# Scheduler priority for the scores and the reads of a batch in an attention-then-MLP kernel

## The chip, the cores and the metric

The kernel runs on one core of a Trainium2 chip. The metric is the device time of one execution in microseconds (us). A core has five engines that run side by side, each through its own list of instructions in a fixed order: TensorE (PE in the profile; its weight loads are PEld), VectorE (DVE), ScalarE (ACT), GpSimd (POOL) and SyncE (SP, which here issues most of the DMAs). An instruction waits until the work of other engines on which it depends is done, and everything behind it on its engine waits too.

## What is computed

Eight batches (B = 8) with eight heads (H = 8) of 512 tokens (S) and 32 memory states (Ns) of width 64 (D). Each token attends to the states and each state to the tokens; the results, 544 rows of 512 for each batch, go through a two-layer MLP with a squared ReLU (512 to 2048 to 512).

```python
scores = scale * np.matmul(x, state.transpose(0, 1, 3, 2))
...
a /= a.sum(-1, keepdims=True) + 1e-09
xread = np.matmul(a, state)
scores2 = scale * np.matmul(state, x.transpose(0, 1, 3, 2))
...
a2 /= a2.sum(-1, keepdims=True) + 1e-09
sread = np.matmul(a2, x)
...
h = x @ w_in
r = np.maximum(h, 0.0)
g = r * r
return (g @ w_out).astype(np.float32)
```

## The kernel before

**The MLP's products.** Every large product is made of three products of split operands (hi times hi, hi times lo, lo times hi), each with 128x128 weights and 512 columns. The token rows of a batch never exist as `xread`: since `xread` is the product of `a` and `state`, the kernel multiplies `state` with `w_in` first. This gives `z` (line 154, a product with 64x32 weights, in pieces of 512 columns), which is split into `z_hi` and `z_lo`. A unit of the MLP is then `ph` (line 362: six matmuls of `z` with the softmax `a_hi`, `a_lo`), its ReLU `r` on ACT (line 367), the square into `ph` on DVE (line 375), the cast `g_hi` on ACT (line 84) and the rest `g_lo` on DVE (line 87), and two units later the second layer, `po` (line 405: twelve matmuls, eight with `g_hi` and four with `g_lo`). A batch has 16 units.

**The attention of a batch.** Among these stand, once for each batch: `scores` (line 203: eight products `pst` with 64x32 weights in float32, each recorded by the profile as two matmuls), the copy `keep` of `pst` on ACT (line 217), the softmax over the states on DVE and ACT (`turn1` to `turn2`, lines 245 to 278), the softmax over the tokens (`exps2`, lines 225 to 233), the transposes `pt` of the latter (line 311) and `read` (line 323: 32 products `pr` with 128x32 weights in float32, two matmuls each, and then the multiplication `rd` on DVE, line 328).

**Buffers.** PSUM has four buffers for `po`, two for `ph` and one (tag `px`) that `pst`, `pt`, `pr` and the pieces of `z` take in turns: each of them has to wait until the one before has been read out. `g_hi` and `g_lo` have two buffers each.

**What sets the order.** The units of the first part, up to the second visit of batch 0, are ordered by the planner in `begin` and stay as written. Everything behind is recorded unit by unit; `Ahead` spreads the steps of the attention over the units by their due times. A scheduler then orders what was recorded, engine by engine, by its own estimate of when each instruction can start and by priority, which is the place in the recording. It orders single instructions, so that the eight products of `scores` or the 32 of `read` may come apart. `tc.high_priority(offset=HURRY)` with `HURRY = 120` (line 129) lets the instructions in it count as recorded that much earlier. Before the change it stands around the pieces of `z` alone (line 608).

Of the kernel before, what the change touches and what calls it, by code (L numbers as in the profile page):

```python
# [18 lines left out]
def memory_attention_then_relu2_ffn(  # L19
# [21 lines left out]
    nc = tc.nc  # L41
    P = 128
    B, S, C = xn.shape
    D = stP.shape[1] // 2
    H = C // D
    N = stP.shape[2] // (H // 2)
    DM, DF = w_out.shape[1] // 2, w_out.shape[0]
    R = S + N
    NG = H * N // P
    HG = H // NG  # L50
    NCC = DM // P
    NFC = DF // P
    NT = S // P
# [75 lines left out]
    HURRY = 120  # L129
# [38 lines left out]
    state = {}  # L168

    def attention(b):  # L170
        NJ = S // 32
        pair, my = [], {}
# [24 lines left out]

        def scores():
            pst = ps_x.tile([P, NG, S], F32, name="pst", tag="px")
            for j in range(HG):  # L200
                for g in range(NG):
                    rows = slice(g * D, (g + 1) * D)
                    nc.tensor.matmul(  # L203
                        pst[j * N:(j + 1) * N, g, :], lhsT=state[b][rows, j, :],
                        rhs=my["t"][rows, j, :], start=True, stop=True,
                    )
            my["pst"] = pst
            my["q1"] = sb.tile([P, NG, NJ, N], F32, name="q1", bufs=1)
            my["m1"] = sb.tile([P, NG, NJ, 1], F32, name="m1", bufs=2)
            my["s1"] = sb.tile([P, NG, NJ, 1], F32, name="s1", bufs=2)  # L210
            my["at"] = sb.tile([P, NG, S], F32, name="at", bufs=1)
            my["nm2"] = sb.tile([P, NG], F32, name="nm2", bufs=2)
            my["e2"] = sb.tile([P, NG, S], F32, name="e2", bufs=LATE)
            my["s2"] = sb.tile([P, NG], F32, name="s2", bufs=2 * LATE)
# [101 lines left out]

        def read():
            pr = ps_x.tile([P, NG, S], F32, name="pr", tag="px")
            for g in range(NG):
                for t in range(NT):  # L320
                    for j in range(HG):
                        h = g * HG + j
                        nc.tensor.matmul(  # L323
                            pr[j * N:(j + 1) * N, g, :D], lhsT=my["e"][:, g, t, j * N:(j + 1) * N],
                            rhs=my["n"][:, t, h * D:(h + 1) * D], start=t == 0, stop=t == NT - 1,
                        )
            rd = sb.tile([P, NG, D], F32, name="rd", bufs=1)
            nc.vector.tensor_mul(  # L328
                out=rd, in0=pr[:, :, :D], in1=my["s2"].rearrange("p (g o) -> p g o", o=1)
                .broadcast_to([P, NG, D])  # L330
            )
            at = (b % GB) * N
            for j in range(HG):
                nc.gpsimd.tensor_copy(  # L334
                    out=sr[b // GB][at:at + N, j * NG * D:(j + 1) * NG * D],
                    in_=rd[j * N:(j + 1) * N].rearrange("p g d -> p (g d)"),
                )

        steps = dict(
            pad=pad, load_t=load_t, scores=scores, keep=keep, exps2=exps2, load_n=load_n, turn=turn,  # L340
            read=read,
        )
        return pair, steps, [soft(gs) if b < 2 else grouped(*soft(gs)) for gs in halves]
# [558 lines left out]
```

## Time and profile before

| | us |
|---|---|
| median of 3 runs | 684.58 (684.29 to 684.79) |
| the profiled execution | 684.99 |
| its span, first to last instruction | 682.8 |
| PE busy | 653.2 (96%) |
| DVE busy | 368.8 (54%) |
| ACT busy | 289.7 (42%) |
| mean granted TensorE clock | 0.998 |

A busy PE says that a matmul was under way, not that it went at its best rate: matmuls overlap, so their durations add up to more than the time they take. What a matmul costs in a full stream is read from the distance between two starts. In the timeline, the first column is the start in us from the beginning of the span, the second the time until the last of the row's instructions ended, then the engine, the line, the operation with its tiles, weights and shape, and the number of instructions in the row.

### The profile page before, as it was taken

The page shows a single profiled execution, that of the slowest core. Times are in us where ns is not written, and L with a number is a line of the kernel's source. Part 1 is how long each engine was busy: PE and PEld are TensorE (multiplying, and loading weights), DVE is VectorE, ACT ScalarE, POOL GpSimd, SP SyncE. Part 2 cuts the span into 40 slices and gives each one's busy share as a digit, 9 for nine tenths or more (in the row PEclk, how much of TensorE's full clock was granted, in tenths as well). Part 3 has the DMA queues.
Part 4 walks back from the last instruction along what each step waited for, and adds up shares of the span by engine and source line. Part 5 has one row for each costly group of instructions (what it writes and reads, how often), then busy time and mean ns, then how long its engine had stood idle before and what let it go on. Part 6 is the DMA issues. An engine that isn't in the chain of part 4 may idle for free.

```text
span 682.8 us, 9542 instructions
## 1 busy us (share of the span) xinstructions
PE 653.2 (96%) x3864; PEld 493.7 (72%) x3864; DVE 368.8 (54%) x522; ACT 289.7 (42%) x468; POOL 24.3 (4%) x44
## 2 busy tenths in 40 slices
PE   1798999999999999999999999999999999999996
PEld 0465876777777777777777876777678767788895
DVE  4899789347557335633473336633483244343553
ACT  3667665334435333523343334423353143333442
POOL 0000000000101000100001000100001000000000
PEclk9999999999999999999999999999999999999999
DMA  8534560023130005000320005000301001000101
GB/s 315 185 127 182 184 232 24 1 70 121 47 138 5 1 1 186 4 1 1 117 69 5 1 1 186 0 1 1 124 0 63 1 0 62 1 0 1 62 1 31
DMA packets 15803, 43.59 MB, mean 64 GB/s; under 512 B 1296, under 2 KB 3344, under 8 KB 13840
## 3 DMA queue, kind: packets, MB, share of 16 engines
q1 hardware_dynamic: 15568, 42.73, 17.3%
q8 instruction: 30, 0.49, 0.3%
q10 hardware_dynamic: 192, 0.26, 0.2%
q14 instruction: 13, 0.11, 0.0%
HBM read 34.08 MB, written 8.91 MB: 63 GB/s over the span
## 4 chain that ended last, share of the span: by engine, by line
PE 90%; DVE 6%; issue 1%; ACT 1%; DMA 1%; SPq 0%; DVEq 0%; ACTq 0%
PE po L405 53%; PE ph L362 28%; PE pz L154 4%; PE pst L203 2%; PE pr L323 1%; PE pt L311 1%; DMA xt_raw<-xT 1%; DVE wof L114 1%; DVE wo_lo L87 1%; DVE z_lo L87 1%; DVE wi L114 1%; DVE wi L120 1%; DVE a_lo L87 0%; DVE q L275 0%; DVE m L251 0%
## 5 line engine op out<-in xcount | busy, mean ns | idle before, releaser
L405 PE MATMUL po<-wo_hi,g_hi 128*128 128x512 f32 x544 | 215.8, 397 | 0.1
L405 PE MATMUL po<-wo_lo,g_hi 128*128 128x512 f32 x544 | 213.9, 393 | 0.8 <-DVE wo_lo L87 0.8
L375 DVE TENSOR_TENSOR ph<-ph,r 128x512 f32<-128x512 f32 (+1 forms) x128 | 84.9, 663 | 138.5 <-ACT r L367 138.4
L367 ACT ACTIVATE r<-ph 128x512 f32<-128x512 f32 (+1 forms) x144 | 82.9, 575 | 177.1 <-PE ph L362 176.7
L405 PE MATMUL po<-wo_hi,g_lo 128*128 128x512 f32 x544 | 154.3, 393 | 0.0
L87 DVE TENSOR_TENSOR g_lo<-ph,g_hi 128x512 fp32r<-128x512 f32 (+1 forms) x144 | 94.8, 658 | 80.4 <-ACT g_hi L84 55.7
L84 ACT CAST g_hi<-ph 128x512 fp32r<-128x512 f32 (+1 forms) x144 | 81.2, 564 | 116.1 <-DVE ph L375 76.8
L405 PEld LDWEIGHTS po<-wo_hi,g_hi 128*128 128x128 f32 x544 | 102.3, 188 | 31.9 <-ACT r L367 5.9
L405 PEld LDWEIGHTS po<-wo_lo,g_hi 128*128 128x128 f32 x544 | 102.2, 188 | 27.5 <-issue 5.0
L405 PEld LDWEIGHTS po<-wo_hi,g_lo 128*128 128x128 f32 x544 | 100.7, 188 | 24.8 <-issue 3.8
L362 PE MATMUL ph<-a_hi,z_hi 128*128 128x512 f32 x256 | 83.9, 409 | 2.6 <-ACT a_hi L84 1.8
L362 PE MATMUL ph<-a_hi,z_lo 128*128 128x512 f32 x256 | 82.6, 402 | 3.4 <-DVE z_lo L87 3.4
L362 PE MATMUL ph<-a_lo,z_hi 128*128 128x512 f32 x256 | 80.7, 397 | 0.0
L362 PEld LDWEIGHTS ph<-a_hi,z_hi 128*128 128x128 f32 x256 | 47.1, 191 | 25.3 <-issue 5.8
L87 DVE TENSOR_TENSOR z_lo<-pz,z_hi 128x1024 fp32r<-128x1024 f32 (+2 forms) x37 | 39.7, 1077 | 46.0 <-ACT z_hi L84 46.0
L362 PEld LDWEIGHTS ph<-a_hi,z_lo 128*128 128x128 f32 x256 | 48.4, 191 | 20.2 <-issue 5.0
L362 PEld LDWEIGHTS ph<-a_lo,z_hi 128*128 128x128 f32 x256 | 48.9, 191 | 10.9
L84 ACT CAST z_hi<-pz 128x1024 fp32r<-128x1024 f32 (+2 forms) x37 | 32.9, 899 | 48.1 <-PE ph L362 26.7
L154 PE MATMUL pz<-wi,sp_raw 64*32 64x512 f32 (+2 forms) x560 | 36.4, 579 | 10.6 <-DVE wi L120 8.6
L154 PEld LDWEIGHTS pz<-wi,sp_raw 64*32 64x32 f32 x560 | 6.5, 107 | 25.1 <-DVE wi L120 10.2
L334 POOL COPY sr<-rd 32x128 f32<-32x128 f32 x32 | 9.2, 288 | 377.0 <-DVE rd L328 376.0
L203 PE MATMUL pst<-xt_raw,sp_raw 64*32 64x512 f32 x128 | 13.7, 658 | 6.6 <-DMA xt_raw<-xT 6.6
(61 smaller groups left out, 383.8 us busy)
## 6 DMA issues: line engine op xcount, KB each, us to landing
xt_raw<-xT SPq DMA_DIRECT2D x8, 1024.0 KB, 4.8
wo_raw<-w_out SPq DMA_DIRECT2D x8, 1024.0 KB, 5.6
xn_raw<-xn SPq DMA_DIRECT2D x8, 1024.0 KB, 5.4
out<-sum SPq DMA_DIRECT2D x32, 256.0 KB, 3.9
wi_raw<-w_in SPq DMA_DIRECT2D x7, 1024.0 KB, 4.8
wi_raw<-w_in SPq DMA_DIRECT2D x2, 512.0 KB, 6.7
sp_raw<-stP SPq DMA_DIRECT2D x8, 64.0 KB, 1.8
out<-os__5348 SPq DMA_DIRECT2D x2, 64.0 KB, 1.7
```

The source lines that it names most:

```text
L84: nc.scalar.copy(out=hi, in_=src)
L87: eng_lo.tensor_sub(out=lo, in0=src, in1=hi.bitcast(F32))
L114: nc.vector.scalar_tensor_tensor(out=bits, in0=high, scalar=-0x80000000, in1=bits, op0=ALU.bitwise_and, op1=ALU.bitwise_or,)
L120: mark[:] = [nc.vector.scalar_tensor_tensor(out=bits, in0=low, scalar=29, in1=bits, op0=ALU.logical_shift_right, op1=ALU.bitwise_or,)]
L154: nc.tensor.matmul(pz[g][j * N:(j + 1) * N], lhsT=state[b][rows, j, :], rhs=wi[rows, j, cols], start=True, stop=True,)
L203: nc.tensor.matmul(pst[j * N:(j + 1) * N, g, :], lhsT=state[b][rows, j, :], rhs=my["t"][rows, j, :], start=True, stop=True,)
L311: nc.tensor.transpose(out=pt[:, g, t, :], in_=my["e2"][:, g, t * P:(t + 1) * P], identity=ident)
L334: nc.gpsimd.tensor_copy(out=sr[b // GB][at:at + N, j * NG * D:(j + 1) * NG * D], in_=rd[j * N:(j + 1) * N].rearrange("p g d -> p (g d)"),)
L362: nc.tensor.matmul(ph, lhsT=w, rhs=v, start=m == 0, stop=m == len(todo) - 1)
L367: nc.scalar.activation(r, my[0], AF.Relu)
L375: nc.vector.tensor_mul(out=ph, in0=ph, in1=r)
L405: nc.tensor.matmul(po[t], lhsT=g, rhs=w, start=i == 0 and j == 0, stop=i == last and j == 2)
```

## The change

The loops of matmuls in `scores` and in `read` are put into `tc.high_priority(offset=HURRY)`. Nothing else is touched; the same instructions are issued. The lines behind shift by one and by two (203 to 204, 323 to 325, 362 to 364, 405 to 407).

```diff
         def scores():
             pst = ps_x.tile([P, NG, S], F32, name="pst", tag="px")
-            for j in range(HG):
-                for g in range(NG):
-                    rows = slice(g * D, (g + 1) * D)
-                    nc.tensor.matmul(
-                        pst[j * N:(j + 1) * N, g, :], lhsT=state[b][rows, j, :],
-                        rhs=my["t"][rows, j, :], start=True, stop=True,
-                    )
+            with tc.high_priority(offset=HURRY):
+                for j in range(HG):
+                    for g in range(NG):
+                        rows = slice(g * D, (g + 1) * D)
+                        nc.tensor.matmul(
+                            pst[j * N:(j + 1) * N, g, :], lhsT=state[b][rows, j, :],
+                            rhs=my["t"][rows, j, :], start=True, stop=True,
+                        )
...
         def read():
             pr = ps_x.tile([P, NG, S], F32, name="pr", tag="px")
-            for g in range(NG):
-                for t in range(NT):
-                    for j in range(HG):
-                        h = g * HG + j
-                        nc.tensor.matmul(
+            with tc.high_priority(offset=HURRY):
+                for g in range(NG):
+                    for t in range(NT):
+                        for j in range(HG):
+                            h = g * HG + j
+                            nc.tensor.matmul(
...
```

**The read, on PE.** This is what stands on PE around the read of batch 2 before, with the numbers of the buffers behind the names (`pr_2019` is the read, `ph_1992` a unit's first layer, `po0` to `po3` the four rows of its second):

```order
L405 MATMUL po3_1529<-wo_hi_76,g_lo_1912 128x512
L323 MATMUL pr_2019<-xn_raw_1967,e_t_1990 32x64 x8
L362 MATMUL ph_1992<-a_hi_1506,z_hi_1876 128x512 x2
L362 MATMUL ph_1992<-a_hi_1506,z_lo_1877 128x512 x2
L362 MATMUL ph_1992<-a_lo_1507,z_hi_1876 128x512 x2
L323 MATMUL pr_2019<-xn_raw_1967,e_t_1990 32x64 x24
L405 MATMUL po0_1526<-wo_hi_76,g_hi_1937 128x512
```

The same place of PE after the change:

```order
L407 MATMUL po3_1529<-wo_hi_76,g_lo_1912 128x512
L325 MATMUL pr_2019<-xn_raw_1967,e_t_1990 32x64 x32
L364 MATMUL ph_1992<-a_hi_1506,z_hi_1876 128x512 x2
L364 MATMUL ph_1992<-a_hi_1506,z_lo_1877 128x512 x2
L364 MATMUL ph_1992<-a_lo_1507,z_hi_1876 128x512 x2
L407 MATMUL po0_1526<-wo_hi_76,g_hi_1937 128x512
```

The 32 products stand in one piece, and `ph_1992` behind all of them. The reads of batches 2 to 5 were split like this, 8 and 24; those of the other batches are whole before and after.

**The scores, on PE.** One second layer further on, before the change, come the scores of batch 4 (`pst_2115`). Six of them stand behind `ph_2083`:

```order
L362 MATMUL ph_2083<-a_hi_1506,z_hi_1876 128x512 x2
L362 MATMUL ph_2083<-a_hi_1506,z_lo_1877 128x512 x2
L362 MATMUL ph_2083<-a_lo_1507,z_hi_1876 128x512 x2
L203 MATMUL pst_2115<-xt_raw_2097,sp_raw_2081 32x512 x6
L405 MATMUL po0_2099<-wo_hi_76,g_hi_1963 128x512
```

The other two stand on PE behind the twelve products of the next second layer, of which the last two are shown:

```order
L405 MATMUL po3_2102<-wo_lo_77,g_hi_1963 128x512
L405 MATMUL po3_2102<-wo_hi_76,g_lo_1964 128x512
L203 MATMUL pst_2115<-xt_raw_2097,sp_raw_2081 32x512 x2
L362 MATMUL ph_2131<-a_hi_1506,z_hi_1876 128x512 x2
L362 MATMUL ph_2131<-a_hi_1506,z_lo_1877 128x512 x2
```

After the change, on PE at the first of these places:

```order
L364 MATMUL ph_2083<-a_hi_1506,z_hi_1876 128x512 x2
L364 MATMUL ph_2083<-a_hi_1506,z_lo_1877 128x512
L204 MATMUL pst_2115<-xt_raw_2097,sp_raw_2081 32x512 x8
L364 MATMUL ph_2083<-a_hi_1506,z_lo_1877 128x512
L364 MATMUL ph_2083<-a_lo_1507,z_hi_1876 128x512 x2
L407 MATMUL po0_2099<-wo_hi_76,g_hi_1963 128x512
```

All eight scores now stand together, in the middle of `ph_2083`. The scores of batches 4 to 7 were split like this, 6 and 2; those of batches 0 to 3 are whole before and after. In all, pieces of small products stand at 69 places of PE's list before and at 61 after. Behind each of the four places, some pieces of `z` and some `ph` stand a few matmuls earlier or later, each still in one piece; in the last batches a `pt` that was split 2 and 6 is split 6 and 2.

**What follows from the scores, on DVE.** Before, DVE takes the transposition of the scores (`q1_2124`) behind the square and the rest of the unit `ph_2083`:

```order
L87 TENSOR_TENSOR g_lo_2003<-ph_1992,g_hi_2002 128x512
L375 TENSOR_TENSOR ph_2083<-ph_2083,r_2090 128x512
L87 TENSOR_TENSOR g_lo_2094<-ph_2083,g_hi_2093 128x512
L245 STREAM_TRANSPOSE q1_2124<-pst_2115 128x1024
L225 TENSOR_REDUCE nm2_2128<-e2_2129 128x2
L375 TENSOR_TENSOR ph_2131<-ph_2131,r_2138 128x512
L251 TENSOR_REDUCE m1_2125<-q1_2124 128x32
```

After the change DVE has there:

```order
L87 TENSOR_TENSOR g_lo_2003<-ph_1992,g_hi_2002 128x512
L246 STREAM_TRANSPOSE q1_2124<-pst_2115 128x1024
L226 TENSOR_REDUCE nm2_2128<-e2_2129 128x2
L377 TENSOR_TENSOR ph_2083<-ph_2083,r_2090 128x512
L252 TENSOR_REDUCE m1_2125<-q1_2124 128x32
L227 TENSOR_SCALAR nm2_2128<-nm2_2128 128x2
L87 TENSOR_TENSOR g_lo_2094<-ph_2083,g_hi_2093 128x512
```

The chain of the scores moved ahead of one unit's square and rest. On ACT the copy `keep` moved ahead of the ReLU and the cast of the same unit (`r_2090`, `g_hi_2093`). The lists of POOL and SP are the same before and after.

More of the change, by code (lines that the diff above doesn't have):

```diff
@@ L318, in read @@
             pr = ps_x.tile([P, NG, S], F32, name="pr", tag="px")
-            for g in range(NG):
-                for t in range(NT):
-                    for j in range(HG):
-                        h = g * HG + j
[L323 to L326, printed above, removed]
+            with tc.high_priority(offset=HURRY):
[4 more added lines that the diff above has]
+                            nc.tensor.matmul(
+                                pr[j * N:(j + 1) * N, g, :D], lhsT=my["e"][:, g, t, j * N:(j + 1) * N],
+                                rhs=my["n"][:, t, h * D:(h + 1) * D], start=t == 0, stop=t == NT - 1,
+                            )
             rd = sb.tile([P, NG, D], F32, name="rd", bufs=1)
```

## The prediction

> **What bounds the kernel now.** I read the page's shares first, then PE's waits without the start, and then how PE's time goes in the stretch where the change moves anything.
>
> ```profile
> PE 653.2 (96%) x3864; PEld 493.7 (72%) x3864; DVE 368.8 (54%) x522; ACT 289.7 (42%) x468; POOL 24.3 (4%) x44
> PE 90%; DVE 6%; issue 1%; ACT 1%; DMA 1%; SPq 0%; DVEq 0%; ACTq 0%
> PE ph L362 <- DVE z_lo L87: 1.1, 1, 1.1
> PE pz L154 <- DVE z_lo L87: 0.4, 1, 0.4
> 240.00:540.00 300.00, 300.00 (x1859) 223.48 (x1858) 143.91 (x202) 114.96 (x182) 16.55 (x28) 1.00 0.12 43
> ```
>
> The second line is the chain that ended last: 90% PE. The third and fourth are all that PE waited for others after 110 us (1.5 us in two waits). The last is the busy time from 240 to 540 us, where all four changed places lie: PE 300.00 of 300 us at a granted clock of 1.00, DVE and ACT under half. So here the end is set by how many matmuls PE starts and at what distance; a gain is a start-to-start distance that goes away, and nothing else is worth anything unless PE begins to wait.
>
> **The price of a step.** In the rows quoted below, 22 matmuls of 128x512 start between 268.37 and 273.41 (four of `ph`, then twelve and six of `po`): 5.04/22 = 0.229 us each. What a piece of small products costs is the distance around it, less 0.229 for each large matmul in that distance.
>
> **The reads.** A read in one piece, of batch 0, and then the split one of batch 2:
>
> ```profile
> 149.99 1.08 PE L405 MATMUL po<-wo_hi,g_lo 128*128 128x512 f32 x4
> 151.00 1.10 PE L323 MATMUL pr<-xn_raw,e_t 128*32 128x64 f32 x64
> 152.03 0.74 PE L362 MATMUL ph<-a_hi,z_hi 128*128 128x512 f32 x2
> 152.61 0.63 PE L362 MATMUL ph<-a_hi,z_lo 128*128 128x512 f32 x2
> ```
>
> ```profile
> 254.77 1.08 PE L405 MATMUL po<-wo_hi,g_lo 128*128 128x512 f32 x4
> 255.78 0.43 PE L323 MATMUL pr<-xn_raw,e_t 128*32 128x64 f32 x16
> 256.14 0.73 PE L362 MATMUL ph<-a_hi,z_hi 128*128 128x512 f32 x2
> 256.71 0.62 PE L362 MATMUL ph<-a_hi,z_lo 128*128 128x512 f32 x2
> 257.17 0.63 PE L362 MATMUL ph<-a_lo,z_hi 128*128 128x512 f32 x2
> 257.72 0.88 PE L323 MATMUL pr<-xn_raw,e_t 128*32 128x64 f32 x48
> 258.53 0.50 PE L405 MATMUL po<-wo_hi,g_hi 128*128 128x512 f32 x1
> 258.87 0.39 PE L405 MATMUL po<-wo_lo,g_hi 128*128 128x512 f32 x1
> ```
>
> Whole: 149.99 to 152.61 is 2.62; six large matmuls are 1.37; the read costs 1.25. Its body is 1.03 (151.00 to 152.03); the rest is paid at the borders: 151.00 is 0.09 later than four steps, and the two `ph` behind take 0.58 for 0.46. Split: 254.77 to 256.71 is 1.94, less 1.37 = 0.57; 257.17 to 258.87 is 1.70, less three steps (0.69) = 1.01; together 1.58. **One read made whole saves 0.33 us**, a pair of borders and 0.14 of body.
>
> **The scores.** Scores in one piece, inside a `ph`, of batch 2:
>
> ```profile
> 156.96 0.40 PE L362 MATMUL ph<-a_hi,z_hi 128*128 128x512 f32 x1
> 157.29 1.09 PE L203 MATMUL pst<-xt_raw,sp_raw 64*32 64x512 f32 x16
> 158.31 0.50 PE L362 MATMUL ph<-a_hi,z_hi 128*128 128x512 f32 x1
> 158.65 0.63 PE L362 MATMUL ph<-a_hi,z_lo 128*128 128x512 f32 x2
> ```
>
> The split ones of batch 4, and the unit `ph_2159` that comes later at 273.41:
>
> ```profile
> 262.31 0.62 PE L362 MATMUL ph<-a_lo,z_hi 128*128 128x512 f32 x2
> 262.87 1.08 PE L203 MATMUL pst<-xt_raw,sp_raw 64*32 64x512 f32 x12
> 263.87 0.50 PE L405 MATMUL po<-wo_hi,g_hi 128*128 128x512 f32 x1
> 264.20 0.39 PE L405 MATMUL po<-wo_lo,g_hi 128*128 128x512 f32 x1
> ...
> 266.51 0.39 PE L405 MATMUL po<-wo_hi,g_lo 128*128 128x512 f32 x1
> 266.82 1.05 PE L203 MATMUL pst<-xt_raw,sp_raw 64*32 64x512 f32 x4
> 267.80 0.72 PE L362 MATMUL ph<-a_hi,z_hi 128*128 128x512 f32 x2
> 268.37 0.63 PE L362 MATMUL ph<-a_hi,z_lo 128*128 128x512 f32 x2
> ...
> 273.41 0.62 PE L362 MATMUL ph<-a_hi,z_hi 128*128 128x512 f32 x2
> ```
>
> This is the larger term. The last two products take 0.98 us of body (266.82 to 267.80), nearly as much as six (1.00) or eight (1.02): up to eight of them run beside one another, so a piece costs the same however few are in it. With its borders the small piece costs 268.37 - 266.51 - 0.69 = 1.17; the six cost 264.20 - 262.31 - 0.69 = 1.20; eight in one piece 158.65 - 156.96 - 0.46 = 1.23. **Scores made whole save 1.17 + 1.20 - 1.23 = 1.14 us.**
>
> **The sum.** The four places are alike: PE's time in scores is the same in each (first and last of four such stretches):
>
> ```profile
> 250.00:280.00 30.00, 2.12 (x16) 1.00 0.31 107
> 475.00:505.00 30.00, 2.12 (x16) 1.00 0.19 71
> ```
>
> So 4 x (0.33 + 1.14) = 5.9 us. Starts are read to 0.01 us and each difference uses several; I allow 0.03 on each of the eight pieces, 5.7 to 6.1. The other moved pieces (`z`, `pt`) stay one piece each, at nothing; 69 places become 61, exactly these eight. The profiled execution had 684.99, of which 2.2 lie outside the span and stay: 684.99 - 5.9 = 679.1. It lies 0.41 over the median of the three runs, 684.58, so the forecast for a median is **678.7**.
>
> A rule of the Trainium skill bears on the borders, and by it the gain would be larger. "TensorEngine Tiling (Array Packing)", section Tiling Modes, says that changing the tiling mode drains TensorE; "TensorE: Matmul & The Clock Gate", section Single matmul latency, puts the drain at some 175 ns. At that price twice per piece, an estimate from that page, a pair of borders would be 0.35 us. The rows have 0.09 to 0.10 on entry and 0.10 to 0.12 on exit, some 0.2 in all, so the drain is there but mostly hidden, and I count the rows.
>
> **What could be late instead.** The scores now come ahead of `ph_2083`'s last three matmuls, and `keep`, `q` and `nm` ahead of its ReLU, square and `g_lo`. Queued behind them is the unit, and PE needs `g_lo_2094` at `ph_2159`, which takes the same PSUM buffer. Rows of before (ACT, then DVE):
>
> ```profile
> 267.92 1.02 ACT L217 COPY e<-pst 128x1024 f32<-128x1024 f32 x1 [0.63 <-PE pst L203]
> 272.02 0.59 ACT L84 CAST g_hi<-ph 128x512 fp32r<-128x512 f32 x1 [1.87 <-DVE ph L375]
> ```
>
> ```profile
> 261.99 0.69 DVE L87 TENSOR_TENSOR g_lo<-ph,g_hi 128x512 fp32r<-128x512 f32 x1 [0.39 <-ACT g_hi L84]
> ...
> 268.97 1.25 DVE L245 STREAM_TRANSPOSE q<-pst 128x1024 f32<-128x1024 f32 x1 [0.95 <-ACT e L217]
> 270.14 1.18 DVE L225 TENSOR_REDUCE nm<-e 128x2 f32<-128x1024 f32 x1
> 271.24 0.69 DVE L375 TENSOR_TENSOR ph<-ph,r 128x512 f32<-128x512 f32 x1
> 271.84 1.21 DVE L251 TENSOR_REDUCE m<-q 128x32 f32<-128x1024 f32 x1
> 273.03 0.68 DVE L87 TENSOR_TENSOR g_lo<-ph,g_hi 128x512 fp32r<-128x512 f32 x1
> ```
>
> The new order has the same sequence one unit earlier, so these distances serve. PE: the read starts at 255.78 as before and `ph_2083` at 261.07; three steps and a border later `pst` at 261.85, done at 262.88. `keep` then starts 0.12 after the piece (267.92 against 267.80), at 263.00; `q` 1.05 later, 264.05; `g_lo_2094` 4.06 after that, 268.11, done at **268.8**; `g_hi_2093` 4.10 after `keep`, 267.1, done at 267.7. Between 262.88 and `ph_2159` PE has 36 large matmuls (three of `ph`, twelve of `po`, six of `ph`, fifteen of `po`; 8.24) and one piece of `z`, priced like scores (1.23 with its borders), besides the scores' exit (0.11): **272.5**. The slack is 3.7 us; `g_hi_2093` is needed three matmuls earlier, at 271.8, with a slack of 4.1. One unit on, `g_lo_2142` has behind `g_lo_2094` on DVE two passes of about 1.2 like that of `m`, a square, and a wait for the exponentials on ACT (about 1.0, like `e`), some 4.1 us to 272.9, and is needed 20 matmuls after 272.5, at 277.0: slack 4.1. The piece of `z`, moved ahead to about 269.9, needs `q` finished, 265.3. At the read, `ph_1992` starts 0.67 later (256.81), and its square goes behind one of the old batch's sums, a pass of the square's shape (0.69): its `g_lo_2003`, done at 262.68 before, comes at 264.1 at worst, and `ph_2131` needs it 15 matmuls after the scores, at 262.88 + 0.11 + 3.44 = 266.4. DMA: SP's list is unchanged, and loads of the next `xt_raw` wait for scores that end five us earlier. I price all this at nothing; if the cover were gone, each us that `g_lo_2094` comes after 272.5 costs 1 us at each of four places.
>
> **Rivals.**
> *The chain on DVE becomes PE's bound (slower).* The point is a `g_lo_2094` later than 272.5. Were the rest of the softmax also run ahead of it, five passes of about 1.2 us, it would come 6.0 later: 2.3 us of wait at each place, 9.2 in all, less 5.9, gives **687.9**. Against it: the order has only `q`, `nm` and `m` ahead. 4%.
> *Part is given back.* A wait of 0.7 us at each place, if the slack of 3.7 is overstated by 4.4: 678.7 + 2.8 = **681.5**. DVE's rows from 268.97 stand back to back, which speaks for it. 7%.
> *Eight scores don't pack beside a `ph` as they do at 157.29.* If the fourth pair took its own 0.98 again, only borders and read are saved, 4 x (0.19 + 0.33) = 2.1: **682.5**. The row at 157.29 speaks against it. 2%.
> *It does nothing.* Were the split pieces hidden behind something else, **684.6**; PE's 300.00 of 300 us says no. 3%.
> *Each border costs a whole drain.* A large matmul lasts 0.39 and the next starts after 0.229, so 0.16 is still under way; if each border waited that out, a pair would cost 0.32 instead of 0.2, and eight pairs 1.0 more: **677.7**. The borders in the rows, at most 0.12, speak against it. 4%. This is the case in which the drain of the Trainium skill's tiling page shows in full.
>
> **How the numbers follow.** The forecast has the remaining 80%. Its own width is 0.2 for the sum and 0.3 for the runs' spread (684.29 to 684.79). The range takes in the drained borders below and part of the waits above: 677.4 to 680.6; what it leaves out, the slower rival, the packing, nothing gained and most of the larger waits, is some 15%. About 0.2%, or 1.4 us, is what a measurement here can tell from no change: faster than 683.2 are the forecast, the drain, the waits and the packing, 93%; within, 3%; slower 4%.
>
> **What would show it.** In the profile after: PE's piece of 16 `pst` with a body of 1.02, 64 `pr` with 1.03 at all four places, PE at 100% from 240 to 535 us, and everything behind the fourth place 5.9 us earlier. Against it: a wait of PE `ph` for DVE `g_lo` near the scores, or a body of `pst` near 2 us.

## The result, and the profile after

The change takes 678.57 us (median of 4 runs, 678.34 to 678.89) against 684.53 (684.29 to 684.79) for the kernel before: 0.9913 of it, 95% interval 0.9896 to 0.993, or 5.96 us less. The forecast was 678.7. The profiled execution of the change took 678.34, with a span of 676.2.

The page after, the engines' busy line; then all that PE waited for after 110 us; then the busy time from 240 to 540 us:

```profile
PE 646.4 (96%) x3864; PEld 492.8 (73%) x3864; DVE 368.0 (54%) x522; ACT 288.9 (43%) x468; POOL 24.3 (4%) x44
```

```profile
PE ph L364 <- DVE z_lo L87: 1.1, 1, 1.1
PE pz L154 <- DVE z_lo L87: 0.4, 1, 0.4
```

```profile
240.00:540.00 300.00, 300.00 (x1896) 227.40 (x1895) 144.35 (x203) 114.85 (x183) 16.53 (x28) 1.00 0.12 43
```

PE is still never without work in the stretch, and behind 110 us it waits for the same two things as before and no longer. It starts more matmuls in the same 300 us: 1896 were recorded against 1859. (The counts are of records, of which a few can be missing.) No wait took the place of what was removed.

PE's timeline of the change at the read of batch 2 and the scores of batch 4, and `ph_2159`, the unit that the prediction watched:

```profile
254.04 1.08 PE L407 MATMUL po<-wo_hi,g_lo 128*128 128x512 f32 x4
255.05 1.10 PE L325 MATMUL pr<-xn_raw,e_t 128*32 128x64 f32 x64
256.08 0.74 PE L364 MATMUL ph<-a_hi,z_hi 128*128 128x512 f32 x2
256.66 0.63 PE L364 MATMUL ph<-a_hi,z_lo 128*128 128x512 f32 x2
...
260.78 0.40 PE L364 MATMUL ph<-a_hi,z_lo 128*128 128x512 f32 x1
261.11 1.09 PE L204 MATMUL pst<-xt_raw,sp_raw 64*32 64x512 f32 x16
262.13 0.50 PE L364 MATMUL ph<-a_hi,z_lo 128*128 128x512 f32 x1
262.47 0.63 PE L364 MATMUL ph<-a_lo,z_hi 128*128 128x512 f32 x2
...
271.72 0.62 PE L364 MATMUL ph<-a_hi,z_hi 128*128 128x512 f32 x2
```

A step is the 0.229 us between the starts of two large matmuls in a full stream. The read now costs 256.66 - 254.04 less six steps = 1.25 us, where the split one cost 1.58. The scores cost 262.47 - 260.78 less two steps = 1.23, where the two pieces cost 2.37. Both are what the whole ones of batches 0 and 2 cost before. The four places are alike; PE's time in scores in the first and the last stretch of 30 us:

```profile
245.00:275.00 30.00, 1.09 (x16) 1.00 0.30 107
470.00:500.00 30.00, 1.09 (x16) 1.00 0.20 71
```

It was 2.12 in each such stretch before.

To compare whole traces I use a distance on PE that leaves the start out: from the piece of `z` that starts at 134.28 us before (133.54 after) to the last transposes, of `sr`, at 606.75 (600.12). The two starts are called marks below. The distance was 472.47 us and is 466.58: **5.89 less**, where the sum forecast 5.9.

### The profile page after: what moved, and what is told of

It is laid out like the page before. It is cut to its first block, busy times and chain, and to the rows that moved or that the text cites. A ratio compares the mean times of both kernels' runs of the same rounds, so it can differ in the third digit from the quotient of the medians.

```text
span 676.2 us, 9543 instructions
## 1 busy us (share of the span) xinstructions
PE 646.4 (96%) x3864; PEld 492.8 (73%) x3864; DVE 368.0 (54%) x522; ACT 288.9 (43%) x468; POOL 24.3 (4%) x44
## 4 chain that ended last, share of the span: by engine, by line
PE 89%; DVE 7%; issue 1%; ACT 1%; DMA 1%; SPq 0%; DVEq 0%; ACTq 0%
PE po L407 53%; PE ph L364 28%; PE pz L154 4%; PE pr L325 1%; PE pst L204 1%; PE pt L312 1%; DVE wof L114 1%; DMA xt_raw<-xT 1%; DVE wo_lo L87 1%; DVE z_lo L87 1%; DVE wi L114 1%; DVE wi L120 1%; DVE wi L108 0%; DVE g_lo L87 0%; DVE a_lo L87 0%
## 5 line engine op out<-in xcount | busy, mean ns | idle before, releaser
L364 PE MATMUL ph<-a_hi,z_hi 128*128 128x512 f32 x256 | 82.4, 403 | 3.0 <-ACT a_hi L84 2.0
L246 DVE STREAM_TRANSPOSE q<-pst 128x1024 f32<-128x1024 f32 (+1 forms) x9 | 10.1, 1126 | 19.7 <-ACT e L218 11.1
```

What stands on the lines that cost most here:

```text
L246: nc.vector.transpose(out=my["q1"][:, gs].rearrange("p g j n -> p (g j n)"), in_=my["pst"][:, gs].rearrange("p g s -> p (g s)"),)
L364: nc.tensor.matmul(ph, lhsT=w, rhs=v, start=m == 0, stop=m == len(todo) - 1)
```

## The experiments

Medians, and the same distance in each profiled execution. The first two rows are from the comparison above. The kernel before was run again beside the others: its median was 684.31 beside the first four of them and 684.30 beside the last three, and the ratios below are to these.

| kernel | median, us | distance on PE, us | against before | against the change |
|---|---|---|---|---|
| before | 684.53 | 606.75 - 134.28 = 472.47 | | |
| the change | 678.57 | 600.12 - 133.54 = 466.58 | -5.89 | |
| scores alone | 679.41 | 602.00 - 134.22 = 467.78 | -4.69 | +1.20 |
| reads alone | 682.14 | 604.56 - 133.40 = 471.16 | -1.31 | +4.58 |
| transposes too | 677.24 | 599.24 - 133.48 = 465.76 | -6.71 | -0.82 |
| scores in two pieces | 682.43 | 604.22 - 133.60 = 470.62 | -1.85 | +4.04 |
| scores in three pieces | 686.73 | 608.70 - 133.48 = 475.22 | +2.75 | +8.64 |
| maxima four times as long | 677.14 | 599.26 - 133.43 = 465.83 | -6.64 | -0.75 |
| maxima seven times as long | 685.64 | 607.13 - 133.37 = 473.76 | +1.29 | +7.18 |

### One half of the change at a time

The diff of the change with its second half left out:

```diff
         def scores():
             pst = ps_x.tile([P, NG, S], F32, name="pst", tag="px")
-            for j in range(HG):
...
+            with tc.high_priority(offset=HURRY):
+                for j in range(HG):
...
```

> The priority stands around the scores alone; the reads of batches 2 to 5 stay split 8 and 24. If the gain is the sum of pieces that go away (theory), this keeps 4 x 1.14 = 4.6 us of it: 684.5 - 4.6 = 679.9. If the order of the chain on DVE and ACT had a part in it, or the pieces were worth the same each (rival), it would be near half, 681.6. In the profile: scores 1.09 us of PE at each of the four places, reads with two pieces as before.

The median was 679.41 (ratio 0.9932, 0.992 to 0.9945), the distance 4.69 shorter, where four scores were to give 4.6; half of the gain is out. PE's timeline has the read of batch 2 still in its two pieces, at 255.72 and 257.66, and the scores of batch 4 in one, at 262.80.

The other half alone:

```diff
         def read():
             pr = ps_x.tile([P, NG, S], F32, name="pr", tag="px")
-            for g in range(NG):
...
+            with tc.high_priority(offset=HURRY):
+                for g in range(NG):
...
```

> The priority stands around the reads alone; the scores of batches 4 to 7 stay split 6 and 2. Theory: 4 x 0.33 = 1.3 us, 683.2. Rival of equal pieces: near half of the gain, 681.6. The two parts together should give the 5.9 to 6.0 of the change within 0.5, as nothing waits.

The median was 682.14 (0.9973, 0.9961 to 0.9984), the distance 1.31 shorter: the forecast term. The medians moved by more, 684.31 - 682.14 = 2.2, and by them alone the rival's 681.6 is nearer than the theory's 683.2; it is the distance, which holds all the reads and scores that differ, that decides for the theory. In the profiled executions the excess lies ahead of the first mark (133.40 against 134.28), at the start of the program, which is taken up at the end; where it lies in the other executions is not shown. The two distances add up to 6.0 against 5.89, so whatever the parts do to each other is some 0.1 us. Pieces are not worth the same: four pieces of scores gave 4.69, four splits of a read 1.31.

### What a piece of scores costs

From batch 2 on, the scores are recorded as two steps one slot apart, and an edge of order puts the second behind a product of the MLP. Those of batches 2 and 3 come in one piece on PE all the same (156.61 and 197.03), so that the four batches 4 to 7 are split:

```diff
...
+        def scores_part(js):
+            with tc.high_priority(offset=HURRY), (
+                tc.issue_after(last_mm[0].ins) if js[0] else ExitStack()
+            ):
+                for j in js:
...
-        steps = [w["pad"], w["load_t"], w["scores"], w["keep"], *p, w["exps2"]]
+        steps = [w["pad"], w["load_t"], w["scores"], *w["rest"], w["keep"], *p, w["exps2"]]
```

> The change with the scores of batches 4 to 7 held apart in two pieces of four, a second layer's products between. Theory: a piece of scores costs about 1.0 us of body and 0.2 of borders however few products are in it, so each extra piece costs 1.17: 678.6 + 4 x 1.17 = 683.3. Rival, the body goes with the number of products and only the borders are paid twice: 678.6 + 4 x 0.2 = 679.4.

PE's timeline at the scores of batch 4, in two pieces of four:

```profile
260.83 0.40 PE L375 MATMUL ph<-a_hi,z_lo 128*128 128x512 f32 x1
261.16 1.06 PE L206 MATMUL pst<-xt_raw,sp_raw 64*32 64x512 f32 x8
262.15 0.50 PE L375 MATMUL ph<-a_hi,z_lo 128*128 128x512 f32 x1
262.49 0.63 PE L375 MATMUL ph<-a_lo,z_hi 128*128 128x512 f32 x2
...
265.70 0.40 PE L418 MATMUL po<-wo_hi,g_lo 128*128 128x512 f32 x1
266.03 1.06 PE L206 MATMUL pst<-xt_raw,sp_raw 64*32 64x512 f32 x8
267.02 0.74 PE L375 MATMUL ph<-a_hi,z_hi 128*128 128x512 f32 x2
267.60 0.63 PE L375 MATMUL ph<-a_hi,z_lo 128*128 128x512 f32 x2
```

Each piece of four has a body of 0.99 and costs 1.20 and 1.21 with its borders, 1.18 more than the whole in the change. The distance grew by 4.04 instead of 4 x 1.17 = 4.68; the missing 0.64 is about what a stall near the end of the change costs, which this order doesn't have (0.67, next experiment). The rival, 0.8 for borders alone, is out. One of the nine executions took 1667.63 us, for a reason that no trace here shows; the other eight took 680.85 to 682.84.

The same with pieces of two, two and four (`PIECES = 4`, of which the last two came together):

> As the run with two pieces of four, with three pieces (two, two and four products) at each of the four places. Theory: two extra pieces at 1.17 each, 678.6 + 8 x 1.17 = 688.0. Rival, only the borders are paid again: 678.6 + 8 x 0.2 = 680.2.

```profile
261.04 1.05 PE L206 MATMUL pst<-xt_raw,sp_raw 64*32 64x512 f32 x4
262.02 0.50 PE L375 MATMUL ph<-a_hi,z_lo 128*128 128x512 f32 x1
...
266.36 1.05 PE L206 MATMUL pst<-xt_raw,sp_raw 64*32 64x512 f32 x4
267.34 0.73 PE L375 MATMUL ph<-a_hi,z_hi 128*128 128x512 f32 x2
...
270.98 1.06 PE L206 MATMUL pst<-xt_raw,sp_raw 64*32 64x512 f32 x8
271.98 0.50 PE L418 MATMUL po<-wo_hi,g_hi 128*128 128x512 f32 x1
```

Bodies of 0.98, 0.98 and 1.00 for two, two and four products. The distance grew by 8.64, against 8 x 1.17 - 0.67 = 8.7; this order doesn't have the stall either. It is slower than the kernel before (1.0038, 1.0023 to 1.0053). So a piece of scores costs some 1.2 us whether it holds two products or eight. The trace of the change shows why: eight matmuls of `pst` are already under way between 261.10 and 261.20, all sixteen between 261.60 and 261.70, and each lasts 0.60. They do run beside one another; in the small piece before, two and then four are under way at once, for the same 0.60 each. With that, the number of pieces alone moves the kernel from 0.4% slower to 0.9% faster.

### The transposes too

The change with the same priority around the transposes `pt`, of which two were still split:

```diff
         def turn():
             pt = ps_x.tile([P, NG, NT, P], F32, name="pt", tag="px")
-            for g in range(NG):
-                for t in range(NT):
...
+            with tc.high_priority(offset=HURRY):
+                for g in range(NG):
+                    for t in range(NT):
...
```

> The change with the transposes pt under the same priority: the two of them that are still split (7 and 1, 6 and 2) become whole, 61 places to 59. Theory: a pt has 128x128 weights like the large products, its pieces pay no entry and some 0.1 us at the exit, so this is worth 0.0 to 0.2 us: 678.4 to 678.6. Rival, each piece is worth a pair of borders or more whatever its weights: 0.4 to 1.2 us, 677.4 to 678.2.

The median was 677.24 (0.9897 of before, 0.9883 to 0.991), and the distance 0.82 below the change: by the numbers the rival's. The trace says otherwise. First the split `pt` of the change, then the whole one:

```profile
174.50 0.93 PE L312 MATMUL pt<-ident,e 128*128 128x128 f32 x7
175.18 0.48 PE L407 MATMUL po<-wo_hi,g_hi 128*128 128x512 f32 x1
...
178.96 0.27 PE L312 MATMUL pt<-ident,e 128*128 128x128 f32 x1
178.98 0.47 PE L407 MATMUL po<-wo_hi,g_hi 128*128 128x512 f32 x1
```

```profile
173.06 1.03 PE L313 MATMUL pt<-ident,e 128*128 128x128 f32 x8
173.85 0.47 PE L408 MATMUL po<-wo_hi,g_hi 128*128 128x512 f32 x1
```

Seven take 0.68, one 0.02, eight 0.79: the single one costs little more than its exit of 0.1 (178.98 to 179.30 is 0.32), and the whole loses as much in its body. From the first mark to the read of batch 2, which holds this place, the two kernels differ by 0.05 (255.05 - 133.54 against 254.94 - 133.48). The gain is all in the last batch, where the other order of the transposes also spread the pieces of `z`. PE there in the change, then with the transposes whole:

```profile
541.26 0.62 PE L364 MATMUL ph<-a_lo,z_hi 128*128 128x512 f32 x2
542.28 1.09 PE L154 MATMUL pz<-wi,sp_raw 64*32 64x512 f32 x16 [0.40 <-DVE z_lo L87]
543.50 0.51 PE L407 MATMUL po<-wo_hi,g_hi 128*128 128x512 f32 x1
543.84 0.40 PE L407 MATMUL po<-wo_lo,g_hi 128*128 128x512 f32 x1
```

```profile
540.63 1.07 PE L408 MATMUL po<-wo_hi,g_lo 128*128 128x512 f32 x4
541.64 1.09 PE L154 MATMUL pz<-wi,sp_raw 64*32 64x512 f32 x16
542.66 0.50 PE L408 MATMUL po<-wo_hi,g_hi 128*128 128x512 f32 x1
542.99 0.39 PE L408 MATMUL po<-wo_lo,g_hi 128*128 128x512 f32 x1
```

In the change this piece of `z` comes 3.5 us behind the one before (538.75) and waits until that one has been read out of the shared PSUM buffer. It costs 543.84 - 541.26 less three steps = 1.89; without the wait 542.99 - 540.63 less five steps = 1.22. That is 0.67 of the 0.82; the other 0.15 is within the 0.0 to 0.2 of the theory. So the theory was right on the transposes, and the kernel is faster for a reason that neither theory named. Among the kernels without added work it is the fastest.

### How much slack the chain on DVE has

The pass that takes the maxima over the states reads its input four, then seven times in batches 4 to 7; the result is the same. It stands ahead of the unit's `g_lo` on DVE.

```diff
+                if b > 3:
+                    nc.vector.tensor_reduce(
+                        out=flat(my["m1"])[:, :, 0],
+                        in_=flat(my["q1"]).rearrange("p j (o n) -> p j o n", o=1)
+                        .broadcast_to([P, n * NJ, LONG, N]), axis=AX.XY, op=ALU.max,
+                    )
+                    return
```

> The change with the pass that takes the maxima over the states (tensor_reduce on DVE) made four times as long in batches 4 to 7, the same result from three more readings of its input. It stands ahead of the unit's g_lo, which comes 3 x 1.1 = 3.4 us later. Here ph_2159 stands five products later on PE than in the change, so the slack is 3.7 + 1.1 = 4.8 us. Theory: no wait, 678.6 within 0.8. Rival, the slack is smaller than worked out or PE feels the chain otherwise: some us more, up to 4 x 3.4, 692.

The median was 677.14 (0.9898 of before, 0.9882 to 0.9915), and PE had no wait for `g_lo`. The pass took 4.41 us instead of 1.21, so 12.8 us of added work on DVE in four batches cost nothing. It is even 0.75 below the change in distance. Here too the last pieces of `z` came further apart and the stall is gone, which is 0.67 of it; the place of the remaining 0.08 isn't shown.

> The same pass seven times as long: g_lo 6 x 1.1 = 6.8 us later, over the slack of 4.8. Theory: PE waits some 2.0 us for DVE g_lo at each of four places, 678.6 + 8 = 686.6 (6 to 12 more, as units behind may wait too). Rival, the chain on DVE has no hold on PE: 678.6.

The median was 685.64 (1.002, 1.0011 to 1.0029), the distance 7.18 more than that of the change. What PE waited for, DVE at the first place (the long pass and `g_lo_2094`), and PE:

```profile
PE ph L372 <- DVE g_lo L87: 6.1, 4, 1.5
```

```profile
266.05 7.61 DVE L254 TENSOR_REDUCE m<-q 128x32 f32<-128x7168 f32 x1
...
273.64 0.69 DVE L87 TENSOR_TENSOR g_lo<-ph,g_hi 128x512 fp32r<-128x512 f32 x1
```

```profile
272.46 0.39 PE L415 MATMUL po<-wo_lo,g_hi 128*128 128x512 f32 x1
274.38 0.74 PE L372 MATMUL ph<-a_hi,z_hi 128*128 128x512 f32 x2 [1.53 <-DVE g_lo L87]
274.95 0.62 PE L372 MATMUL ph<-a_hi,z_lo 128*128 128x512 f32 x2
```

Four waits of 1.5 us, one at each place, and for the instruction that the prediction named. The mechanism of the slower rival exists, with its point between the two lengths. The pass is 6.4 us longer than in the change and delays PE by 1.69 here (272.46 to 274.38 less a step), which leaves a slack of 4.7, near the 4.8 worked out for this order. In the change, where `ph_2159` stands five products earlier, some 3.6 of it are left.

## Why the prediction was right

**The bound.** PE's starts set the end before and after; 5.89 us fewer on PE between the marks go with 5.96 fewer in the median. That these two agree to 0.1, and the median with the forecast, is in part luck: the profiled executions moved by 6.65, of which 0.74 arose ahead of the first mark, where no term of the sum lies, and against the later medians of the kernel before, 684.31 and 684.30, the gain would be 5.7.

**The terms.** Reads: 0.33 each, 1.31 measured for four alone. Scores: 1.14 each, 4.6 for four, 4.69 measured alone. The allowance of 5.7 to 6.1 holds the distance, and the difference of the medians too.

**The reason.** That a small piece of scores costs as much as a whole was read from one pair of rows (0.98 and 1.02); the runs in two and three pieces show it for two, four, six and eight products (0.98, 0.99 to 1.00, 1.00, 1.02), and the matmuls under way at once show that they run beside one another.

**The cover.** The forecast for the chain was worked out from distances of the kernel before. In the change, ACT's copy of the scores and the cast, then DVE's transposition and `g_lo_2094`:

```profile
262.31 1.02 ACT L218 COPY e<-pst 128x1024 f32<-128x1024 f32 x1 [0.94 <-PE pst L204]
...
266.41 0.59 ACT L84 CAST g_hi<-ph 128x512 fp32r<-128x512 f32 x1 [2.58 <-DVE ph L377]
```

```profile
263.36 1.25 DVE L246 STREAM_TRANSPOSE q<-pst 128x1024 f32<-128x1024 f32 x1 [1.75 <-ACT e L218]
...
267.41 0.69 DVE L87 TENSOR_TENSOR g_lo<-ph,g_hi 128x512 fp32r<-128x512 f32 x1
```

`g_lo` starts 5.10 behind the copy (5.11 forecast) and is done at 268.1; `ph_2159` starts at 271.72. The slack is 3.6 (3.7 forecast). The experiments with the longer pass bracket it in their own order, where it is 1.1 larger.

**The rivals.** Packing beside a `ph`: a body of 1.02, as elsewhere. Whole drains: entry 0.10 and exit 0.11 in the change (261.11 is 0.10 later than one step behind 260.78, and 262.13 to 262.47 is 0.34, a step and 0.11), 0.2 for a pair, so it is out. The larger gain by the drain figure of the Trainium skill ("TensorE: Matmul & The Clock Gate", section Single matmul latency) is out with it: its estimate was 0.35 for a pair. Part given back: PE has no new wait. Nothing gained: the distance is 5.89 shorter.

**What it missed.** The stall of a piece of `z` at 548.92 before and at 542.28 after was in the rows that were quoted (0.4 us, after 110 us) and was left as it is. It was worth more than the wait shown, 0.67, and could be had: it's most of what the version with whole transposes gains.

## What to carry to other kernels

Where PE is never idle, look at how far apart its matmuls start, not at how long it is busy: small products that run beside one another on parts of the array should be issued in one piece, since here two of them cost nearly the same time as eight (0.98 and 1.02). Before a product is moved ahead, take the distances of its chain from the trace as it is and set them against the next use on PE; this gave the slack to 0.1 us. Where a scheduler decides the order, a change in one place moves others, so a gain has to be looked up where it arose before it is put down to the edit.

## What the runs showed that was not expected

**A wait costs more than its record.** In the longest version each wait was recorded with 1.53, but 272.46 to 274.38 is 1.69 over a step and the next pair has 0.57 for 0.46: 1.80 lost, and 4 x 1.80 = 7.2 is the 7.18 by which the distance grew. The piece of `z` recorded 0.40 and lost 0.67. The recorded wait begins only when the last matmul has ended, 0.16 after the next one would have started in a full stream, and the first pair behind the wait loses another 0.11: 1.53 + 0.16 + 0.11 = 1.80. The piece of `z` starts 0.46 later than without the wait (542.28 against 541.26, two steps and an entry of 0.10), and its body is 1.22 (to 543.50) for 1.02.

**The start varies.** The profiled executions differ by 684.99 - 678.34 = 6.65, more than the 5.89. Of the other 0.76, 0.74 arose ahead of the first mark (134.28 - 133.54). PE's timeline before, then after, early in the program:

```profile
29.71 1.05 PE L362 MATMUL ph<-a_hi,z_hi 128*128 128x512 f32 x2
30.57 1.05 PE L362 MATMUL ph<-a_hi,z_lo 128*128 128x512 f32 x2
31.42 0.98 PE L362 MATMUL ph<-a_lo,z_hi 128*128 128x512 f32 x2
```

```profile
29.61 0.70 PE L364 MATMUL ph<-a_hi,z_hi 128*128 128x512 f32 x2
30.16 0.62 PE L364 MATMUL ph<-a_hi,z_lo 128*128 128x512 f32 x2
30.62 0.62 PE L364 MATMUL ph<-a_lo,z_hi 128*128 128x512 f32 x2
```

In the profile before nearly all of these start 0.43 us apart (29.71 to 30.57 for two), in the one after 0.28 and then 0.23; the turn to full speed came some six matmuls earlier there, in an order that the change doesn't touch. The traces have it in the granted clock: its record begins, at full speed, 32.18 us into the span before and 29.75 after. (The clock column of the profile shows 1.00 ahead of that too, where nothing is on record.) Of the nine profiled executions the kernel before and the one with scores alone turned last, at 32.2, the others at 29.3 to 30.6; these two also have the latest first marks, 134.28 and 134.22 against 133.37 to 133.60. The Trainium skill's "TensorE: Matmul & The Clock Gate", section What's actually happening, describes such a half-speed start that ends at a point which varies from run to run; the steps agree with it. That it differs by the run and not by the kernel wasn't tested.
